# Three rotating buffers in place of two for the packed halves of f, q, k and k's gated product

## The chip, the cores and the metric

The kernel runs on one core of a Trainium2 chip. Its time is the device time of one execution in microseconds (us), as a median over several runs. Durations inside the kernel come from one profiled execution of the same program.

## The reference

The kernel computes a gated linear attention (B = 4 batches, H = 8 heads, S = 768 steps, D = 48 per head) and after it a layer norm and a two-layer MLP with a residual:

```python
f = 1.0 / (1.0 + np.exp(-f_logit))
for t in range(S):
    state = f[:, :, t, :, None] * state + np.einsum('bhd,bhe->bhde', k[:, :, t], v[:, :, t])
    y[:, :, t] = np.einsum('bhd,bhde->bhe', q[:, :, t], state)
x = y.transpose(0, 2, 1, 3).reshape(B, S, H * D)
xn = (x - mu) / np.sqrt(var + 1e-06) * g_ln
out = x + np.maximum(xn @ w_ch1, 0.0) @ w_ch2       # w_ch1: 384 x 1536, w_ch2: 1536 x 384
```

## The kernel before

The sequence is cut into NU = 12 units of T = 64 steps; a unit holds all four batches, so 256 tokens. For each unit n there is an attention part, `attention(n)`, and an MLP part, `mlp(n)`. No planner orders the work: the program runs through a plan written out by hand as a string of tokens, `START` for the first units and then `UNIT` once for each m from 3 to 11. Each token issues the instructions of one step, and each engine and each DMA queue executes its instructions in the order of the plan. An engine waits (on a semaphore) where an operand or a buffer is not ready; everything behind the waiting instruction on that engine waits too. A round of `UNIT` interleaves the MLP of unit m with the attention of unit n = m+1, the gates, q and k of unit o = m+2, and the fetching of unit p = m+3.

The matmuls need f, q and k with the head dimension across the partitions. The first three units do this with transposes on TensorE. From unit 3 on (`DIRECT = 3`) it is done by DMA, and a DMA transposition moves elements of 2 bytes, so each 4-byte number goes as two packed halves:

1. the raw tensor is loaded by DMA (`fraw`, or `kraw` for k and, in turn, for q);
2. `split(n, name, i, queue)`, line 420: ScalarE (ACT) copies one half of the rows (i = 0 or 1) into a tile `planes` (line 439), the low and the high 16 bits apart, and a DMA writes that tile to a DRAM tile, `{name}halves` (line 440). A token `p...` issues this DMA on GpSimd's queue (POOL), a token `P...` on SyncE's (SP);
3. `transfer(n, name)`, line 442, token `x...`: a DMA transposition on SP (line 454) brings both halves back from DRAM, turned, into `turned` (f and q share that tile) or into the tile named `qraw` (used for k). It waits for both writes.

The same is done with `kh`, k times its gates (name `K`), whose turned form `kt` the state update needs (`do_kt`).

So there are eight copies into `planes` in each round: two each for q, k, f and K. In the plan of a round their tokens are, in order: `p{p}f1`, `P{o}q0`, `p{o}q1`, `p{p}f0`, `p{p}k1`, `P{p}k0`, `p{o}K1`, `p{o}K0`. All take their tile from the pool `raws` under one tag, and with it one of that tag's buffers; a copy waits until the DMA that reads the buffer's former content has landed. The framework decides at build time which buffer a tile gets.

Around them, in the order of the plan on each engine: ACT also does the relus of `by_blocks` (line 962; the MLP's first product as blocks in DVE-made combinations), the copies of the attention's result into x (lines 816, 818), the copy of the first partial product p1 (line 1066), the sigmoid of the gates (line 695) and the scaled eviction of the transposed x (line 888). VectorE (DVE) adds partial products (lines 959, 1001, 1059), does the statistics (830, 831), the sums s1 to s4 of h (`sums`, lines 930 to 933), qh = turned q times the gates (725), kh (716), the normalization (875), the state (853) and kept, the state that is carried on (738). TensorE (PE) multiplies: `by_blocks` (line 951), then seven products p1, p2, p6, p5, p7, p3, p4 of the second layer (line 1051), with the transposes of x (886) ahead of p4, then the carried term of the next unit (`do_carried`, line 757, reads qh and kept), the scores (771), the values (807) and the state update (845). The one-bank PSUM tiles of all these rotate through four banks (`ps1`, bufs=4).

The third line of a round's plan, as an example:

```python
a{n}.chunk m{m} a{n}.stats m{m} x{o}q s{m} p{p}k1 P{p}k0 L{z}f a{o}.q a{o}.k m{m} x{p}f m{m}
```

Of the kernel before, what the change touches and what calls it, by code (L numbers as in the profile page):

```python
# [12 lines left out]
U16 = mybir.dt.uint16  # L13
# [314 lines left out]
def kernel(  # L328
# [20 lines left out]
    B, H, S, D = q.shape  # L349
    P = 128  # L350
# [31 lines left out]
    raws = fast.enter_context(tc.tile_pool(name="raws", bufs=2))  # L382
# [31 lines left out]
    def raw_of(n, name):  # L414

        return wide_heads["k" if n >= DIRECT and name == "q" else name]
# [3 lines left out]
    def split(n, name, i, queue):  # L420

        if n >= NU or n < DIRECT:
            return
        if (n, name) not in halved:
            halved[n, name] = drams.tile([P, 2, 2, 64 * H], U16, tag=f"{name}halves",
                                         name=f"{name}halves{n}")
        planes = raws.tile([P, 2, 64 * H], U16, tag="planes", name=f"{name}planes{n}_{i}")
        if name == "K":
            src = by_gates[n].rearrange("p (i s) t -> p i (s t)", i=2)[:, i].bitcast(U16).rearrange(
                "p (c two) -> p two c", two=2)  # L430
            to, there = planes, halved[n, name][:, :, i]
        else:
            src = raw_of(n, name).rearrange("p g h e -> p (g h e)")[
                :, i * D:i * D + (H - 1) * R * D + 64]
            src = bass.AP(tensor=src.tensor, offset=src.offset,
                          ap=[src.ap[0], [R * D, H], [1, 64]]).bitcast(U16).rearrange(
                              "p h (c two) -> p two h c", two=2)
            to, there = planes.rearrange("p two (h c) -> p two h c", h=H), halved[n, name][:, i]
        nc.scalar.copy(out=to, in_=src)  # L439
        queue.dma_start(out=there, in_=planes)  # L440
# [660 lines left out]
    def run(plan):  # L1101
        for token in plan.split():
# [8 lines left out]
            elif kind == "m":  # L1111
                if token not in running:
                    running[token] = mlp(int(rest))
                next(running[token])
            elif kind in "lL":
                queues = (nc.scalar if kind == "L" else nc.sync,)
                if rest[-1].isdigit():
                    load(int(rest[:-2]), rest[-2], (int(rest[-1]),), queues)
                else:
                    load(int(rest[:-1]), rest[-1], engines=queues)  # L1120
            elif kind in "pP":
                split(int(rest[:-2]), rest[-2], int(rest[-1]),
                      nc.sync if kind == "P" else nc.gpsimd)
            elif kind == "x":
                transfer(int(rest[:-1]), rest[-1])
            elif kind == "h":
                if token not in running:
                    running[token] = first_half(int(rest[0]), int(rest[1]))
                next(running[token])
            elif kind == "s":  # L1130
                sums(int(rest))
            elif kind == "y":
                if FIRST <= int(rest) < NU:
                    sums_of_x(int(rest))
            else:
                {"r": read, "w": write, "f": fetch, "t": mix, "d": idle,
                 "T": lambda: mix(nc.gpsimd), "u": mix_step,
                 "U": lambda: mix_step(nc.gpsimd)}[token]()
# [54 lines left out]
```

## Time and profile before

| what | value |
|---|---|
| time, median of 3 runs | 434.49 us (433.64 to 435.8) |
| profiled execution: its span | 434.5 us |
| TensorE busy (PE), its weight loads (PEld) | 415.5 us, 387.1 us |
| VectorE (DVE), ScalarE (ACT), GpSimd (POOL) busy | 332.9, 214.6, 121.8 us |
| mean granted TensorE clock | 0.987 |
| copies into planes (line 439) | 18 each for f, q, k and K, about 1.04 us each |
| DMA, all queues | 71.68 MB, mean 165 GB/s |

PE and PEld are one engine's matmuls and weight loads, which overlap. Matmuls are pipelined and their ends are modelled. An engine that is idle lost something only if it is on the path that sets the end. In the lists of waits the column after `<-` names what ended the wait; "issue" stands where the profile shows nothing that was waited for. SPq, ACTq and POOLq are the sequencers that issue DMAs.

### The profile page before, as it was taken

The numbers are of one execution on the slowest core, as the hardware profiler recorded it, in microseconds if no ns is written. First come the engines' busy times: TensorE is split into PE (matmuls) and PEld (weight loads), VectorE is DVE, ScalarE is ACT, GpSimd is POOL, SyncE is SP. The second block draws the span as 40 slices with busy tenths as digits, with TensorE's granted clock in tenths as the row PEclk, the third lists the DMA queues.
The fourth block names the chain that finished last, engine by engine and source line by source line (L and its number), as shares of the span: only waits on it lengthen the run. The fifth ranks groups of instructions, "written<-read, shape, count | busy, mean of one in ns | idle before, by whom it ended". The sixth has DMA issues, their size and how long they took to land.

```text
span 434.5 us, 12953 instructions
## 1 busy us (share of the span) xinstructions
PE 415.5 (96%) x5429; PEld 387.1 (89%) x5429; DVE 332.9 (77%) x539; ACT 214.6 (49%) x364; POOL 121.8 (28%) x148
## 2 busy tenths in 40 slices
PE   5599999899999997999999999999999999999995
PEld 4589887667879987999999999999999999999995
DVE  5998797665886758879879879879979879665561
ACT  2484856442544435665564564564574462351320
POOL 2362453560024004304204205105106005013011
PEclk9699999999999999999999999999999999999999
DMA  9998978896967798888797797698695690401001
GB/s 169 286 222 178 238 234 207 195 223 168 195 139 180 160 187 175 211 211 179 191 214 168 193 218 176 179 217 182 179 216 149 169 171 26 111 2 24 16 9 33
DMA packets 167647, 71.68 MB, mean 165 GB/s; under 512 B 151760, under 2 KB 157840, under 8 KB 167584
## 3 DMA queue, kind: packets, MB, share of 16 engines
q1 hardware_dynamic: 151728, 54.38, 58.5%
q0 software_dynamic: 3872, 12.64, 8.5%
q10 hardware_dynamic: 11984, 3.79, 4.2%
q8 instruction: 44, 0.72, 0.7%
q14 instruction: 19, 0.16, 0.1%
HBM read 28.31 MB, written 23.59 MB: 119 GB/s over the span
## 4 chain that ended last, share of the span: by engine, by line
PE 80%; DVE 6%; issue 5%; DMA 2%; POOL 2%; SPq 2%; ACT 2%; ACTq 0%; POOLq 0%; DVEq 0%
PE pp L1051 27%; PE bx L951 10%; PE by L951 9%; PE ph L1022 7%; PE ph L900 4%; PE po L1032 4%; PE bz L951 3%; PE shared L771 2%; PE py L757 2%; PE py L807 2%; PE bw L951 2%; PE bv L951 2%; PE xp L886 2%; PE shared L845 2%; DMA qhalves<-qplanes 1%
## 5 line engine op out<-in xcount | busy, mean ns | idle before, releaser
L962 ACT ACTIVATE h<-h 128x512 f32<-128x512 f32 x45 | 28.2, 630 | 42.2 <-DVE h L959 36.5
L1051 PE MATMUL pp<-mixed,s 128*128 128x192 f32 x240 | 40.7, 326 | 2.4 <-DVE s L931 2.4
L1051 PE MATMUL pp<-mixed,h 128*128 128x192 f32 x240 | 42.4, 326 | 0.0
L1051 PE MATMUL pp<-w,h 128*128 128x192 f32 x240 | 41.1, 327 | 1.1 <-ACT h L962 1.1
L1051 PEld LDWEIGHTS pp<-mixed,s 128*128 128x128 f32 x240 | 39.2, 190 | 2.6 <-issue 2.6
L1051 PEld LDWEIGHTS pp<-w,h 128*128 128x128 f32 x240 | 38.9, 190 | 1.7 <-ACT h L962 1.4
L1051 PEld LDWEIGHTS pp<-mixed,h 128*128 128x128 f32 x240 | 39.1, 190 | 0.1
L959 DVE TENSOR_TENSOR h<-h,bx 128x512 f32<-128x512 f32 x36 | 24.6, 683 | 17.1 <-PE bx L951 16.4
L439 ACT COPY Kplanes<-kh 128x1024 uint16<-128x1024 uint16 x18 | 18.2, 1045 | 37.8 <-DVE kh L716 26.4
L888 ACT ACTIVATE xt<-xp,gain 128x128 f32<-128x128 f32 x72 | 19.9, 373 | 31.5 <-PE xp L886 31.5
L668 DVE TENSOR_TENSOR_SCAN after<-gates,ends 128x1040 f32<-128x1040 f32 (+1 forms) x13 | 29.8, 2290 | 6.0 <-ACT gates L699 3.4
L1032 PE MATMUL po<-w,h 128*128 128x384 f32 x96 | 32.3, 489 | 0.0
L1022 PE MATMUL ph<-xt,w 128*128 128x256 f32 x144 | 31.9, 380 | 0.0
L440 POOL DMA_DIRECT2D qhalves<-qplanes x9 | 4.9, 545 | 96.5 <-ACT qplanes L439 96.5
L1022 PEld LDWEIGHTS ph<-xt,w 128*128 128x128 f32 x144 | 27.1, 190 | 4.1 <-ACT xt L888 0.3
L951 PE MATMUL bx<-y,v 128*128 128x128 f32 x216 | 28.7, 275 | 0.0
L680 DVE TENSOR_TENSOR_SCAN upto<-gates,starts 128x1040 f32<-128x1040 f32 (+1 forms) x13 | 28.1, 2158 | 0.5
L1032 PEld LDWEIGHTS po<-w,h 128*128 128x128 f32 x96 | 17.8, 190 | 11.3
L951 PEld LDWEIGHTS bx<-y,v 128*128 128x128 f32 x216 | 26.4, 192 | 0.1
L833 POOL TENSOR_SCALAR rstd<-mv 128x2 f32<-128x2 f32 (+1 forms) x13 | 8.1, 626 | 62.2 <-DVE mv L831 61.9
L439 ACT COPY fplanes<-fraw 128x1024 uint16<-128x1024 uint16 x18 | 18.9, 1054 | 8.9 <-DMA qhalves<-qplanes 6.6
L439 ACT COPY kplanes<-kraw 128x1024 uint16<-128x1024 uint16 x18 | 18.2, 1044 | 9.1 <-DMA kraw<-in_k_dram 4.4
(172 smaller groups left out, 955.3 us busy)
## 6 DMA issues: line engine op xcount, KB each, us to landing
w_0words<-in_moe_w_ch_dram SPq DMA_DIRECT2D x7, 768.0 KB, 5.1
v<-in_v_dram SPq DMA_DIRECT2D x46, 96.0 KB, 3.8
Khalves<-Kplanes POOLq DMA_DIRECT2D x16, 256.0 KB, 3.6
kraw<-in_k_dram SPq DMA_DIRECT2D x40, 96.0 KB, 3.8
fhalves<-fplanes POOLq DMA_DIRECT2D x14, 256.0 KB, 3.8
kraw<-in_q_dram SPq DMA_DIRECT2D x36, 96.0 KB, 3.1
fraw<-in_f_logit_dram ACTq DMA_DIRECT2D x27, 96.0 KB, 2.9
khalves<-kplanes POOLq DMA_DIRECT2D x9, 256.0 KB, 3.9
```

The lines of the kernel that those rows point to most:

```text
L439: nc.scalar.copy(out=to, in_=src)
L668: nc.vector.tensor_tensor_scan(out=at["after"].rearrange(flat)[:, c0:c1][:, ::-1], data0=gt[:, c0 + 1:c1 + 1][:, ::-1], data1=ends.rearran ...
L680: nc.vector.tensor_tensor_scan(out=at["upto"].rearrange(flat)[:, c0:c1], data0=gt[:, c0:c1], data1=starts.rearrange(flat)[:, c0:c1], initi ...
L757: nc.tensor.matmul(py[half(b ^ r), r, e * D:(e + 1) * D], lhsT=qh[head_rows(r), 2 * e + b], rhs=kept[head_rows(r), b, e], start=e == 0, st ...
L888: nc.scalar.mul(out=xt[:, m, g * P:(g + 1) * P], in_=pt[:, m], mul=gain[:, m:m + 1])
L900: nc.tensor.matmul(ph[:, j], lhsT=w1[:, m, (i + j) * P:(i + j + 1) * P], rhs=xt[:, m, tokens], start=m == 0, stop=m == KD - 1)
L951: nc.tensor.matmul(banks[bank][:, i], lhsT=right[:, i * P:(i + 1) * P], rhs=left, start=new and i == 0, stop=True, skip_group_check=True)
L959: nc.vector.tensor_tensor(out=out[to], in0=out[to], in1=bank, op=op)
L962: nc.scalar.activation(out=out[to], in_=out[to] if bank is None else bank, func=AF.Relu)
L1022: nc.tensor.matmul(ph[:, j], lhsT=w1[:, m, (i + j) * P:(i + j + 1) * P], rhs=xt[:, m], start=m == 0, stop=m == KD - 1)
L1032: nc.tensor.matmul(po, lhsT=h[:, i, g * P:(g + 1) * P], rhs=w2[:, i], start=i == 0, stop=i == KF - 1)
L1051: nc.tensor.matmul(pp, lhsT=a[:, i], rhs=b[:, i], start=i == 0, stop=i == KH - 1)
```

## The change

The tile `planes` of line 427 gets its own number of buffers, three, where the pool's two held before. No instruction, transfer or order in the plan is changed. One buffer is 2 x 512 numbers of 2 bytes in each of 128 partitions.

```diff
-        planes = raws.tile([P, 2, 64 * H], U16, tag="planes", name=f"{name}planes{n}_{i}")
+        planes = raws.tile([P, 2, 64 * H], U16, tag="planes", bufs=3,
+                           name=f"{name}planes{n}_{i}")
```

## The prediction

> **What bounds the kernel now.** I read the page's busy shares first, then the stretches of the span by engine, then the chain that ended last, then who waited for whom, and last the timeline of the one place that these point to. Busy time by engine, and the stretches (columns: length, then busy time and instructions of PE, PEld, DVE, ACT, POOL, then clock, DMA share, GB/s):
>
> ```profile
> PE 415.5 (96%) x5429; PEld 387.1 (89%) x5429; DVE 332.9 (77%) x539; ACT 214.6 (49%) x364; POOL 121.8 (28%) x148
> ...
> 80.00:140.00 60.00, 58.87 (x620) 46.67 (x619) 43.94 (x64) 26.86 (x44) 20.14 (x22) 1.00 0.79 185
> 140.00:168.38 28.38, 24.88 (x412) 22.73 (x410) 18.76 (x32) 14.33 (x22) 4.13 (x6) 1.00 0.91 170
> 168.38:400.71 232.33, 232.32 (x3253) 228.66 (x3254) 190.21 (x322) 119.31 (x203) 61.80 (x83) 1.00 0.69 163
> ```
>
> From 168.38 to 400.71 us PE is idle for 0.01 us. Whatever ACT waits for in that stretch costs nothing, because PE never runs out of work. ACT's waits can only matter where PE has a hole, and the one hole of size that lies after the first planes copies is in 140 to 168.38: 28.38 - 24.88 = 3.50 us. The chain that ended last (start, length, what) goes through that hole:
>
> ```profile
> 155.21 6.21 DMA qhalves<-qplanes
> ...
> 168.38 8.04 PE pp L1051 x48
> ...
> 177.07 1.95 PE pp L1051 x12
> ```
>
> So the write of a q half to DRAM carries the time of the whole kernel for 6.21 us. The waits (who <- whom: us in total, times, longest) say what stood behind it:
>
> ```profile
> PE pp L1051 <- DVE s L931: 2.4, 1, 2.4
> PE pp L1051 <- ACT h L962: 1.1, 1, 1.1
> PEld pp L1051 <- issue: 2.6, 1, 2.6
> PEld pp L1051 <- ACT h L962: 1.4, 1, 1.4
> ACT fplanes L439 <- DMA qhalves<-qplanes: 6.6, 1, 6.6
> ACT Kplanes L439 <- DMA khalves<-kplanes: 8.6, 2, 4.7
> ```
>
> PE lost 2.4 + 1.1 = 3.5 us in two waits (its weight loads, which stop first, 2.6 + 1.4 = 4.0), once each. ACT's single 6.6 us wait, for a buffer of planes, is the cause: the relu (L962) and the sums s wait behind it. The timeline of unit m=3 on all engines shows the order:
>
> ```profile
> 144.25 0.56 POOL L440 DMA_DIRECT2D fhalves<-fplanes  x1 [2.59 <-ACT fplanes L439]
> ...
> 153.88 1.04 ACT L439 COPY qplanes<-kraw 128x1024 uint16<-128x1024 uint16 x1
> 154.15 0.53 SPq L440 DMA_DIRECT2D qhalves<-qplanes  x1
> 155.21 0.54 POOL L440 DMA_DIRECT2D qhalves<-qplanes  x1 [10.40 <-ACT qplanes L439]
> 157.54 2.02 SPq L474 DMA_DIRECT2D kraw<-in_k_dram  x4
> 161.44 3.25 SPq L454 DMA_TRANSPOSE turned<-qhalves  x1
> 161.50 1.04 ACT L439 COPY fplanes<-fraw 128x1024 uint16<-128x1024 uint16 x1 [6.58 <-DMA qhalves<-qplanes]
> 162.84 0.54 POOL L440 DMA_DIRECT2D fhalves<-fplanes  x1 [7.08 <-ACT fplanes L439]
> 164.96 0.56 DVE L830 BATCH_NORM_STATS2 stats<-x 128x6 f32<-128x384 f32 x1 [4.42 <-ACT x L818]
> 167.30 1.04 ACT L439 COPY kplanes<-kraw 128x1024 uint16<-128x1024 uint16 x1 [1.24 <-issue]
> 169.89 1.61 DVE L725 TENSOR_TENSOR qh<-turned,upto 128x1024 f32<-128x1024 f32 x1
> ```
>
> I call the copies of this unit f1, q0, q1, f0, k1, k0 in ACT's order. f0 could start at 154.92 (q1's copy ends) and starts at 161.50. The DMA issues give the time to landing (last column), of f1's write (issued 144.25), q0's, q1's, then f0's and the transposition of q:
>
> ```profile
> fhalves<-fplanes POOLq DMA_DIRECT2D x1, 256.0 KB, 3.3
> ...
> qhalves<-qplanes SPq DMA_DIRECT2D x1, 256.0 KB, 3.6
> ...
> qhalves<-qplanes POOLq DMA_DIRECT2D x1, 256.0 KB, 6.2
> ...
> fhalves<-fplanes POOLq DMA_DIRECT2D x1, 256.0 KB, 4.4
> turned<-qhalves SPq DMA_TRANSPOSE x1, 6.0
> ...
> turned<-fhalves SPq DMA_TRANSPOSE x9, 4.3
> ...
> turned<-qhalves SPq DMA_TRANSPOSE x9, 5.5
> ```
>
> q0's write landed at 154.15 + 3.6 = 157.75, q1's at 155.21 + 6.2 = 161.4. f0 went at 161.50, so its buffer was the one that q1 had just filled, not the older one. f1's write had landed at 144.25 + 3.3 = 147.6.
>
> **The change part by part.** It adds one buffer of 128x1024 uint16, 2 KB in each partition. It adds and removes no instruction, no DMA and no byte, and changes no engine's order. No wait is added: a copy into planes waits for an older write than before, or for the same one. So everything is in the waits.
>
> First, f0. With three buffers, q0 and q1 hold two and the third is f1's, free since 147.6. f0 starts at 154.95 in place of 161.50. Its write follows on POOL 0.3 us after the copy (162.84 against 162.54 in the rows), so at about 156.3 in place of 162.84. On POOL it stands behind q1's issue (over at 155.75) and ahead of nothing until rstd, after the statistics. Its 256 KB now travel beside the k loads (SP, 157.54) and behind q1's write in POOL's own queue, not beside the transposition of q.
>
> Second, what this frees. Unit m=4 runs the same program without the wait, so it is the ruler:
>
> ```profile
> 160.54 1.47 PE L1051 MATMUL pp<-w,h 128*128 128x192 f32 x8
> 163.13 2.87 PE L1051 MATMUL pp<-w,h 128*128 128x192 f32 x16 [1.12 <-ACT h L962]
> 168.38 4.14 PE L1051 MATMUL pp<-mixed,s 128*128 128x192 f32 x24 [2.38 <-DVE s L931]
> ...
> 178.96 1.15 PE L757 MATMUL py<-kept,qh 48*64 48x48 f32 x64
> ...
> 196.53 4.07 PE L1051 MATMUL pp<-w,h 128*128 128x192 f32 x24
> ...
> 210.94 1.15 PE L757 MATMUL py<-kept,qh 48*64 48x48 f32 x64
> ```
>
> ```profile
> 190.81 1.05 ACT L439 COPY fplanes<-fraw 128x1024 uint16<-128x1024 uint16 x1
> ```
>
> From the first product p1 to the next carried term (L757), unit 3 takes 178.96 - 160.54 = 18.42 us and unit 4 takes 210.94 - 196.53 = 14.41. The difference, 4.01, is the hole as the weight loads see it. In unit 4, f0's copy starts 5.72 us ahead of p1; in the new unit 3 it would start 160.54 - 154.95 = 5.59 ahead: the same place. So the most that can be had is 4.0 us, with the carried term at 174.95.
>
> Third, what is late next. In unit 3 the transposition of q waits for q1's landing, which nothing here moves, so it is still issued at 161.44, while PE's work moves up past it. DVE's qh needs it, and kept, the last thing that the carried term needs, stands behind qh on DVE:
>
> ```profile
> 201.36 1.62 DVE L725 TENSOR_TENSOR qh<-turned,upto 128x1024 f32<-128x1024 f32 x1
> ...
> 208.71 0.95 DVE L738 TENSOR_TENSOR kept<-state,total 128x768 f32<-128x768 f32 x1
> ```
>
> From qh's start to kept's end it is 209.66 - 201.36 = 8.30 us. DVE itself would be ready for qh at 160.54 + (201.36 - 196.53) = 165.37. The landing is bounded by 4.3 us (the other transposition into the same tile) and 6.0 (this very transfer, with f0's write beside it): 165.7 to 167.4. I take 5.5, the median of its kind, since f0's write is now out of its way: 166.94. Then kept ends at 175.24, and the carried term starts there instead of 178.96: 3.7 us gained. At 6.0 it is 175.74 and 3.2; at 166.65 or earlier nothing is left to wait for and it is 4.0.
>
> At that transfer a rule can be weighed. f0's write and the transposition landed 0.2 us apart (162.84 + 4.4 against 161.44 + 6.0). The Trainium skill, DMA: Bandwidth & Descriptors, section Queues, rings and completion order, says that a completion's semaphore write lands only after every earlier write of that DMA engine, across its queues. The two landings agree with it but do not prove it. By that rule the transposition was held up by f0, would now come at its 4.3, and the kernel at 430.5.
>
> Fourth, all other planes copies. ACT's other waits on these buffers (8.6 us for Kplanes, the largest) fall between 80 and 140, where PE lacks 1.13 us in all, or in the full stretch after 168.38. I cost them at nothing; PE's queue of matmuls hides them, and if that cover were gone a copy would be worth at most its own wait. From the carried term on, PE runs without a hole to 400.71, so 3.7 us at 179 are 3.7 at the end, if unit 4 does not find its own transfers late; its q copies stand in ACT's order and move up with it.
>
> The sum: 434.5 - 3.7 = 430.8 us. The profiled span, 434.5, is also the median of the runs shown, 434.49 (433.64 to 435.8).
>
> **The rivals.** *No change.* The wait row shows that a copy does not simply get the oldest buffer: f0 got the newest, with the slower landing. If it got q1's again, nothing moves: 434.5. Against it: f1's buffer has been free for 7 us at that point, and even q0's (157.75) would do, since from f0 to the statistics ACT needs 164.96 - 161.50 = 3.46 us, so 161.2, which delays DVE by less than the wait for q does. *The k loads take its place.* k1's copy waited 1.24 us at 167.30 for something that the page calls issue. If that was the k load (issued at 157.54) and not f0's landing at 167.24, then k1, k0 and ACT's copy of p1 behind them stay where they are, and p1's PSUM bank is free only at about 169.5. Four banks hold p1, p2, p6 and p5; p7 is due at 160.54 + 4 x 1.95 = 168.3 and would be 1.2 late: carried at 176.15, 2.8 gained, 431.7. Against it: 167.24 and 167.30 fit too well, and with three buffers k1 no longer needs f0's. *Slower.* f0's 256 KB go out while q1's write, the k loads and the transpositions are under way. If that holds up the transposition of q, all of DVE stands behind it. The break-even is a landing at 178.96 - 8.30 = 170.66, 9.2 us after its issue; slower by 0.5% needs 11.4. At 12 us the carried term would start at 181.7 and the kernel end at 437.3. Against it: none of the landings quoted is over 6.2.
>
> **How the numbers follow.** Forecast 0.60: 430.8, its own range 430.0 to 432.0 (the landing's bounds, 430.5 to 431.3, and half a microsecond or so of run to run spread). k loads 0.12: 431.7. No change 0.20: 434.5 with the spread of the runs. Slower 0.06: about 437. Other 0.02. A measurement of this kernel tells about 0.5% (2.2 us) from nothing. Faster by over that: the forecast almost whole and most of the k case, 0.68; within it 0.26; slower 0.06. To hold 8 in 10, the range takes the first two cases and the lower half of no change: 429.8 to 434.6.
>
> **What would show it.** Right: f0's copy starts within 0.1 us of q1's copy's end; the 6.6 us row of ACT is gone; PE's two waits on pp (2.4 and 1.1) are gone or under 0.5; unit 3 from p1 to the carried term takes 14.4 to 15.3 us; from there on the times are those of before less the gain; qh is the one that waits, for the transposition of q. Wrong: f0 still waits for a q write; or k1 becomes ACT's long wait; or a hole of the same size opens further on, in unit 4, where PE has none now; or the first p1 is no longer at about 160.5, which would mean that the copies between 80 and 140 were not free.

## The result and the profile after

The changed kernel takes 431.85 us (median of 22 runs) against 435.19 us (median of 22 runs of the kernel before, on the same chip): a ratio of 0.994, interval 0.9916 to 0.9963 (the medians are over all runs; the ratio leaves out those that were disturbed and is not the quotient of the two medians, which is 0.9923). The forecast was 430.8 us, with a range of 429.8 to 434.6.

In the changed kernel every line from 428 on has a number one higher (the copy into planes is L440, its write L441, the products L1052, the carried term L758). The profiled execution took 431.19 us, of which its span is 429.4. First the busy row of its page, and the row of the chain that ended last, by engine:

```profile
PE 414.6 (97%) x5429; PEld 386.7 (90%) x5429; DVE 335.2 (78%) x539; ACT 214.2 (50%) x364; POOL 120.7 (28%) x148
...
PE 88%; ACT 3%; DVE 2%; SPq 2%; DMA 2%; issue 1%; POOL 0%; ACTq 0%; DVEq 0%; POOLq 0%
```

The same row of the kernel before, for comparison:

```profile
PE 80%; DVE 6%; issue 5%; DMA 2%; POOL 2%; SPq 2%; ACT 2%; ACTq 0%; POOLq 0%; DVEq 0%
```

Each engine has about as much to do as before (PE 415.5 us, now 414.6; DVE 332.9, now 335.2); PE's part of the chain has grown from 80% to 88%. The stretches of the span (length, then busy time and instructions of PE, PEld, DVE, ACT, POOL, then clock and DMA) show where:

```profile
80.00:140.00 60.00, 59.52 (x622) 47.12 (x621) 46.94 (x65) 27.35 (x45) 19.65 (x22) 1.00 0.86 190
140.00:164.36 24.36, 24.36 (x412) 22.91 (x412) 19.23 (x31) 14.65 (x22) 5.39 (x8) 1.00 0.91 196
164.36:395.90 231.54, 231.49 (x3252) 227.97 (x3251) 188.25 (x321) 118.52 (x202) 59.54 (x81) 1.00 0.70 162
```

The stretch with the hole, 28.38 us with PE busy for 24.88 of it, is now 24.36 us with PE busy for all of it, and holds the same 412 matmuls. The timeline of unit m=3 shows that the cause is gone. The first fence is PE (the carried term, then p1 and the last product, then the next carried term); the second is ACT, the queues and DVE around the copies:

```profile
142.17 1.15 PE L758 MATMUL py<-kept,qh 48*64 48x48 f32 x64
...
159.75 4.07 PE L1052 MATMUL pp<-w,h 128*128 128x192 f32 x24
163.65 4.06 PE L1052 MATMUL pp<-mixed,s 128*128 128x192 f32 x24
...
174.15 1.15 PE L758 MATMUL py<-kept,qh 48*64 48x48 f32 x64
```

```profile
151.47 0.53 SPq L441 DMA_DIRECT2D qhalves<-qplanes  x1
...
153.09 1.04 ACT L440 COPY qplanes<-kraw 128x1024 uint16<-128x1024 uint16 x1
154.02 1.05 ACT L440 COPY fplanes<-fraw 128x1024 uint16<-128x1024 uint16 x1
154.42 0.54 POOL L441 DMA_DIRECT2D qhalves<-qplanes  x1 [11.79 <-ACT qplanes L440]
154.46 2.09 SPq L475 DMA_DIRECT2D kraw<-in_k_dram  x4
155.36 0.54 POOL L441 DMA_DIRECT2D fhalves<-fplanes  x1 [0.41 <-ACT fplanes L440]
157.69 3.09 SPq L455 DMA_TRANSPOSE turned<-qhalves  x1
161.33 1.05 ACT L440 COPY kplanes<-kraw 128x1024 uint16<-128x1024 uint16 x1 [0.44 <-DMA kraw<-in_k_dram]
...
164.58 1.61 DVE L726 TENSOR_TENSOR qh<-turned,upto 128x1024 f32<-128x1024 f32 x1
```

f0's copy (154.02) follows q1's (153.09) with no wait in brackets; it had waited 6.58 us. From p1 to the next carried term it is 174.15 - 159.75 = 14.40 us, where it was 18.42: the whole 4.0. One thing was not foreseen: the transposition of q is issued at 157.69, not at 161.44. It waits for q1's write, and the landings (last column) of that write and of the transposition show what changed:

```profile
qhalves<-qplanes POOLq DMA_DIRECT2D x1, 256.0 KB, 3.3
...
turned<-qhalves SPq DMA_TRANSPOSE x1, 5.2
```

q1's write, the same 256 KB from the same queue, took 3.3 us and not 6.2. SP's queue was ahead at this time, and on that queue stands the write of another copy, that of K (k times its gates), which no longer waited. Before, then after:

```profile
131.72 1.05 ACT L439 COPY Kplanes<-kh 128x1024 uint16<-128x1024 uint16 x1 [3.83 <-DMA khalves<-kplanes]
132.79 0.59 SPq L440 DMA_DIRECT2D Khalves<-Kplanes  x1
```

```profile
128.19 1.04 ACT L440 COPY Kplanes<-kh 128x1024 uint16<-128x1024 uint16 x1
129.25 0.59 SPq L441 DMA_DIRECT2D Khalves<-Kplanes  x1
```

SP issued K's write 3.5 us earlier, q0's 2.7 earlier (151.47 against 154.15) and the k loads 3.1 earlier (154.46 against 157.54); 0.8 of each is that the whole round began earlier (142.17 against 142.96). That the earlier queue is what shortens q1's write is not shown by this. So the two profiles left three questions. How large is the hole, as profile and runs disagree (4.0 us against 0.6%, 2.6 us)? Is f0's buffer the cause by itself, or does the early K copy carry part of it? And does the third buffer lose something elsewhere, for example in the opening?

### The profile page after: what moved, and what is told of

It reads as the page before. It is cut to its first block, busy times and chain, and to the rows that moved or that the text cites. A ratio compares the mean times of both kernels' runs of the same rounds, so it can differ in the third digit from the quotient of the medians.

```text
span 429.4 us, 12958 instructions
## 1 busy us (share of the span) xinstructions
PE 414.6 (97%) x5429; PEld 386.7 (90%) x5429; DVE 335.2 (78%) x539; ACT 214.2 (50%) x364; POOL 120.7 (28%) x148
## 4 chain that ended last, share of the span: by engine, by line
PE 88%; ACT 3%; DVE 2%; SPq 2%; DMA 2%; issue 1%; POOL 0%; ACTq 0%; DVEq 0%; POOLq 0%
PE pp L1052 32%; PE bx L952 11%; PE by L952 10%; PE ph L1023 7%; PE po L1033 5%; PE bz L952 4%; PE ph L901 3%; PE py L808 2%; PE py L758 2%; PE shared L772 2%; PE bw L952 2%; PE bv L952 2%; SPq L475 2%; PE xp L887 2%; PE shared L846 2%; DMA kraw<-in_k_dram 1%
## 5 line engine op out<-in xcount | busy, mean ns | idle before, releaser
L1052 PE MATMUL pp<-mixed,h 128*128 128x192 f32 x240 | 42.4, 326 | 0.0
L1052 PE MATMUL pp<-w,h 128*128 128x192 f32 x240 | 40.8, 326 | 0.0
L1052 PE MATMUL pp<-mixed,s 128*128 128x192 f32 x240 | 40.6, 326 | 0.0
L1052 PEld LDWEIGHTS pp<-mixed,s 128*128 128x128 f32 x240 | 39.3, 190 | 0.0
L1052 PEld LDWEIGHTS pp<-w,h 128*128 128x128 f32 x240 | 38.9, 190 | 0.3
L1052 PEld LDWEIGHTS pp<-mixed,h 128*128 128x128 f32 x240 | 39.1, 190 | 0.1
L440 ACT COPY Kplanes<-kh 128x1024 uint16<-128x1024 uint16 x18 | 18.2, 1047 | 29.0 <-DVE kh L717 25.2
L441 POOL DMA_DIRECT2D qhalves<-qplanes x9 | 4.9, 545 | 98.4 <-ACT qplanes L440 98.4
L440 ACT COPY kplanes<-kraw 128x1024 uint16<-128x1024 uint16 x18 | 18.3, 1047 | 9.1 <-DMA kraw<-in_k_dram 6.0
L563 POOL TENSOR_TENSOR w<-w_0upper,w_0units 128x768 int32<-128x768 int32 x7 | 14.6, 2082 | 28.6 <-DVE w_0upper L561 28.6
```

The lines of the kernel that those rows point to most:

```text
L563: nc.gpsimd.tensor_tensor(out=to.bitcast(I32), in0=upper, in1=units, op=ALU.add)
L1052: nc.tensor.matmul(pp, lhsT=a[:, i], rhs=b[:, i], start=i == 0, stop=i == KH - 1)
```

## The experiments

In all of them the measure is the round of unit 3: from the carried term that opens it (that of unit 4, PE `py<-kept,qh` at 142 us or so) to the next one. In the changed kernel it is 174.15 - 142.17 = 31.98 us, with PE busy throughout. The kernel before had 36.0. What a round has over 31.98 is called its hole. In the kernels of the experiments the line numbers are one or two higher than before.

**Is the hole a constant?** Both kernels were run again unchanged: the one before three more times (one of them timed over several runs too), the one after three more times (two of them timed over several runs too).

> The kernel before, unchanged, for a second profile of it. Theory A (the hole of unit 3 belongs to the buffer that f0 is given): the 6.6 us wait of ACT and PE's waits of 2.4 and 1.1 us on pp are there again, and from p1 (L1051) to the carried term (L757) unit 3 takes about 18.4 us, within 0.5. Theory B (the hole hangs on how long q1's write takes, which varies from one execution to the next): the wait is of another size, between 2 and 7 us, and unit 3 takes 14.4 us plus 0 to 4.

> The kernel before against itself: what the comparison gives where nothing differs, and a third profile. Unit 3's round took 36.0 and 36.2 us in the two profiles, 4.0 to 4.2 over a round without a hole, but the timed gain of the change is 2 to 3.3 us. Theory C (the hole is of the same size every time, and the rest is the spread of the opening): 35.9 to 36.3 us again, and the moment of the first carried term of unit 4 (141.4 and 143.0 us before) scatters by a microsecond or more; ratio to itself within 0.997 to 1.003. Theory D (the hole varies, and the profiles happened to catch large ones): the round takes under 35 us in this profile or the next.

> A fourth profile of the kernel before. Theory C: unit 3's round 35.9 to 36.3 us. Theory D: under 35 us here or in the third.

The timeline's carried terms, the products with the sums s between them, ACT's wait (us in total, times, longest) and, last, the stretch of these products (columns as above, with the granted clock third from the end) in the first repetition:

```profile
141.44 1.15 PE L757 MATMUL py<-kept,qh 48*64 48x48 f32 x64
...
165.38 5.82 PE L1051 MATMUL pp<-mixed,s 128*128 128x192 f32 x24 [2.29 <-DVE s L931]
...
177.63 1.15 PE L757 MATMUL py<-kept,qh 48*64 48x48 f32 x64
...
ACT fplanes L439 <- DMA qhalves<-qplanes: 5.1, 1, 5.1
...
165.38:171.20 5.82, 5.82 (x26) 5.82 (x27) 5.82 (x9) 1.21 (x3) 2.87 (x4) 0.71 0.56 159
```

The carried terms and the waits of the second:

```profile
143.47 1.15 PE L757 MATMUL py<-kept,qh 48*64 48x48 f32 x64
177.14 1.15 PE L757 MATMUL py<-kept,qh 48*64 48x48 f32 x64
...
ACT fplanes L439 <- DMA qhalves<-qplanes: 4.3, 1, 4.3
PE pp L1051 <- DVE s L931: 1.5, 1, 1.5
```

And of the third:

```profile
143.00 1.15 PE L757 MATMUL py<-kept,qh 48*64 48x48 f32 x64
177.18 1.15 PE L757 MATMUL py<-kept,qh 48*64 48x48 f32 x64
...
ACT fplanes L439 <- DMA qhalves<-qplanes: 4.8, 1, 4.8
PE pp L1051 <- DVE s L931: 2.0, 1, 2.0
```

The rounds are 36.19, 33.67 and 34.18 us, and 36.00 in the profile that the prediction was made from. So the same program has a hole of 4.2, 1.7, 2.2 or 4.0 us, on average 3.0, and not one of a fixed size (theory D, not theory C). Not all of the 4.2 in the first repetition is waiting. There the 24 products with the sums took 5.82 us at a granted clock of 0.71; in the other three profiles they took 4.14 us at 1.00. That is 1.7 us, and no run here shows what lowered the clock. Without it the holes that come from waiting are 4.0, 2.5, 1.7 and 2.2 us, 2.6 on average. Their times were 435.17, 434.56 (median of 12; ratio against itself 0.9982, interval 0.9943 to 1.0021) and 435.97 us. With the clock set apart, f0's wait sets the hole: in each of the four profiles the hole is that wait (6.58, 5.09, 4.26 and 4.76 us) less 2.6 us, and in the three runs below in which f0 waits it is the wait less 2.5 or 2.6. So about 2.6 us of the wait cost nothing, and PE loses what lies beyond them.

> The changed kernel, unchanged, for a second profile and beside the one with a buffer for f0 alone, on one chip. Theory A: the round of unit 3 takes 31.98 us again, ratio to before 0.990 to 0.994, and the same as that of f0's own buffer within 0.2%. Rival (the earlier copies are worth something by themselves): it is faster than f0's own buffer by over 0.2%.

> The changed kernel again. Theory C: unit 3's round 31.98 us, the first carried term of unit 4 anywhere between 141 and 144.5 us, as in the kernel before. Rival E (three buffers slow the opening by about a microsecond, which takes back part of the 4.0): over all profiles the carried term of unit 4 comes 0.8 us or more later in the kernels whose opening has three buffers than in those with two. Ratio 0.991 to 0.996.

> A fourth profile of the changed kernel. Theory C: unit 3's round 31.98 us; the carried term of unit 4 between 141 and 144.5 us. Rival E: it comes late again, at 143.5 us or after.

The changed kernel gave 432.86 us (ratio 0.9955, 0.9921 to 0.9989), 433.76 (0.9943, 0.9911 to 0.9975) and 430.84 in a single execution; for the first the ratio was expected at 0.990 to 0.994. Its round was 31.98 or 31.99 us in all of its four profiles. The hole is what varies, and the third buffer takes away a wait of varying length.

The eight profiles divide as follows (us; the first carried term is that of unit 4 in the timeline, "six rounds" are those from the carried term of unit 5 to that of unit 11, the end is what follows it in the span):

| profile | first carried term | round of unit 3 | six rounds | the end | span |
|---|---|---|---|---|---|
| before, the one shown | 142.96 | 36.00 | 192.37 | 63.2 | 434.5 |
| before, again | 141.44 | 36.19 | 192.58 | 63.2 | 433.4 |
| before, third | 143.47 | 33.67 | 192.58 | 63.1 | 432.8 |
| before, fourth | 143.00 | 34.18 | 192.64 | 64.5 | 434.3 |
| after, the one shown | 142.17 | 31.98 | 192.10 | 63.2 | 429.4 |
| after, again | 143.91 | 31.99 | 191.94 | 63.2 | 431.0 |
| after, third | 141.47 | 31.99 | 192.10 | 63.1 | 428.7 |
| after, fourth | 142.01 | 31.98 | 191.97 | 63.1 | 429.1 |

The mean spans differ by 433.75 - 429.55 = 4.2 us: 0.3 at the first carried term, 3.0 in the round of unit 3 (0.4 of it the low clock of one profile), 0.5 in the six rounds, and 0.3 at the end, where a single profile has 1.3 more, behind PE's last matmul. The rival that three buffers slow the opening finds no support: the first carried term comes at 142.4 on average with three and at 142.7 with two, where 0.8 us or more later was expected. Both scatter by 2 us or more, so the difference of 0.3 between four and four says nothing, and a small effect either way is not excluded.

The runs give less than these spans: 2.0 to 2.6 us by the ratios. None of the profiled executions of the changed kernel (431.19, 432.72, 430.39, 430.84) lies above the median of its set, and the third is the lowest of 12 whose median is 433.76. What the longer runs lose is in no profile. The granted clock goes with part of it: in the third set the longest run, 436.39 us, had a mean of 0.978 and the shortest 0.986; but one of 434.49 us had 0.988, so the rest stays open.

**Is f0's buffer enough?** All tiles keep their two buffers, and f0 of unit 6, the one that waited, gets one of its own:

```diff
+        own = (n, name, i) == (DIRECT + 3, "f", 0)
+        planes = raws.tile([P, 2, 64 * H], U16, tag="ownplanes" if own else "planes",
+                           bufs=1 if own else 2, name=f"{name}planes{n}_{i}")
```

> Two buffers for all copies as before, and one of its own for the single copy f0 of unit 3 (the first half of f of unit 6). Theory A (f0's buffer is all that the third buffer changes): unit 3 from p1 to the carried term falls from 18.4 to 14.4 to 15.3 us; q1's write still lands about 6 us after its issue, so the transposition of q is issued about 1 us after p1 and qh waits for it; ratio to before 0.994, like the full change. Theory B (the earlier copies, which put SP's queue ahead, do it): SP stays where it was, q1's write still lands late, and the ratio stays within 0.998 to 1.002.

> Two buffers and one more for f0 of unit 3 alone, again, beside the full change on one chip. Theory A: round of unit 3 at 31.98 us, ratio within 0.2% of the full change's. Rival: slower than the full change by over 0.2%.

Rows of the timeline and of the landings, first run:

```profile
142.34 1.15 PE L759 MATMUL py<-kept,qh 48*64 48x48 f32 x64
154.19 1.05 ACT L441 COPY fplanes<-fraw 128x1024 uint16<-128x1024 uint16 x1
174.32 1.15 PE L759 MATMUL py<-kept,qh 48*64 48x48 f32 x64
...
qhalves<-qplanes POOLq DMA_DIRECT2D x1, 256.0 KB, 4.3
```

It took 431.36 us (ratio 0.9894, 0.985 to 0.9939, 6 runs) and, run again beside the changed kernel, 432.33 (0.9966, 0.9939 to 0.9992) where that had 0.9955. The round is 31.98 us in both profiles. K's copy still waited (2.69 us in the first), q1's write took 4.3 and 5.7 us, and it made no difference; theory B, by which the earlier copies do it, fails. So f0's own buffer removes the hole whole, and in time the two kernels can't be told apart. In the second run k1's copy waited 2.97 us for the k loads, and PE lost nothing; but it came 4.1 us after p1, where the prediction, with k1 6.8 us after p1, saw p7 late.

**What does the early K copy do?** There are three buffers here too, but the third is shared by three tiles alone: an early K copy, q1 and f0. So f0 must wait for q1's write, as before.

```diff
+        third = (n, name, i) in ((DIRECT, "K", 1), (DIRECT + 2, "q", 1), (DIRECT + 3, "f", 0))
+        planes = raws.tile([P, 2, 64 * H], U16, tag="third" if third else "planes",
+                           bufs=1 if third else 2, name=f"{name}planes{n}_{i}")
```

> The third buffer goes to the second half of K of unit 3 (the copy that waited 3.8 us in the opening) and later to q1 and f0 of unit 3 together, so that f0 still has to wait for q1's write, as before. Theory A (f0's buffer): f0 waits for q1's landing as before, unit 3 takes 17.5 to 18.4 us, ratio 0.998 to 1.002. Theory B (SP's queue ahead): K's copy goes about 3.8 us sooner, SP issues q0's write about 2 us sooner, q1's write lands in about 3.3 us in place of 6.2, f0 waits about 3.5 us in place of 6.6, and unit 3 takes 14.8 to 15.6 us; ratio about 0.995.

I had taken the wrong K: that of unit 3 is copied at about 90 us, and the one at 130.69 belongs to unit 4 and still waited 3.53 us. So it says nothing on an early K, but is a good control: three buffers in memory, f0 tied to q1. Timeline and waits:

```profile
159.85 1.04 ACT L441 COPY fplanes<-fraw 128x1024 uint16<-128x1024 uint16 x1 [6.73 <-DMA qhalves<-qplanes]
...
PE pp L1053 <- DVE s L933: 2.4, 1, 2.4
PE pp L1053 <- ACT h L964: 1.3, 1, 1.3
```

The hole is back, 36.15 - 31.98 = 4.2 us, with the two waits of PE that the kernel before had. The time is 435.12 us (0.9972, 0.9936 to 1.0008). With `(DIRECT + 1, "K", 1)` in the list, the K copy is the right one:

> The run with K tied gave the third buffer to the wrong K (of unit 3, at 92 us), so SP's queue was not ahead in it. Here it goes to the second half of K of unit 4, the copy at about 131 us that waits 3.5 to 3.8 us, and later to q1 and f0 together, so that f0 must still wait for q1's write. Theory A (f0's buffer is the cause; SP's queue matters little): f0 waits at least 5 us, and from one carried term to the next, the round of unit 3 takes 35.5 us or more (31.98 without a hole, 36.0 and 36.2 before). Theory B (SP's queue ahead makes q1's write land in about 3.3 us in place of 4.7 to 6.2): K's copy goes at about 128 us, f0 waits about 3.5 us, the round takes 32.3 to 33.5 us, ratio about 0.995.

```profile
130.06 1.04 ACT L441 COPY Kplanes<-kh 128x1024 uint16<-128x1024 uint16 x1
...
159.93 1.05 ACT L441 COPY fplanes<-fraw 128x1024 uint16<-128x1024 uint16 x1 [3.86 <-DMA qhalves<-qplanes]
...
PE pp L1053 <- DVE s L933: 1.1, 1, 1.1
...
qhalves<-qplanes POOLq DMA_DIRECT2D x1, 256.0 KB, 3.5
```

K didn't wait, q1's write took 3.5 us, f0 waited 3.86, and the round was 33.28: a hole of 1.3. In the profile that is what theory B forecast, and not theory A, which gave SP's queue little weight (a wait of at least 5 us, a round of 35.5 or more). In time it is 433.62 us, 0.998 (0.9951 to 1.001), where theory B had 0.995; the hole's 1.3 us, read from one profile, can't be told from the others in time. Over all profiles of kernels with two or three buffers q1's write took 3.2 to 3.8 us in the five where K had not waited, and 3.9 to 6.9 in the eight where it had. The ranges lie close together without overlapping, so the early K copy probably shortens that write; how it does so was not tried. It matters only while f0 depends on that write.

**Two buffers, strictly in turn.** f0 would then get q0's buffer, whose write is older:

```diff
+        by_gates["count"] = by_gates.get("count", 0) + 1
+        planes = raws.tile([P, 2, 64 * H], U16, tag=f"planes{by_gates['count'] % 2}", bufs=1,
```

> Two buffers as before, but dealt strictly in turn, so that f0 gets q0's buffer and not q1's. No more memory than before. If the choice of the buffer and not the number is what matters: f0 waits only for q0's write (landed 3.6 us after its issue), about 2.8 us in place of 6.6; the statistics come about 0.7 us late, which the transposition of q covers; unit 3 takes 14.4 to 15.3 us and the ratio is 0.994 like that of three buffers. If the number is what matters: unit 3 stays over 17 us and the ratio within 0.998 to 1.002.

```profile
158.22 1.04 ACT L441 COPY fplanes<-fraw 128x1024 uint16<-128x1024 uint16 x1 [3.53 <-DMA qhalves<-qplanes]
...
PE pp L1053 <- DVE s L933: 0.7, 1, 0.7
```

433.05 us, 0.9923 (0.9886 to 0.996, 9 runs). In the profile the wait is 3.53 us and the round 33.05, a hole of 1.1, and the next round has one of 1.0 (33.02), where all four profiles of the kernel before have 31.98. So part of the gain is to be had without memory. By its ratio it is no worse than three buffers, by its profile it is; a single profile of a wait that varies does not decide it.

**One buffer**, to see how far the rest of the program leans on the second:

```diff
-        planes = raws.tile([P, 2, 64 * H], U16, tag="planes", bufs=3,
+        planes = raws.tile([P, 2, 64 * H], U16, tag="planes", bufs=1,
```

> One buffer: each copy into planes waits for the landing of the write before it. It prices the cover in the full stretch, where the waits for two buffers cost nothing. f0 would start about 3.5 us later than with two (q1's write, issued 0.3 us after its copy, lands about 3 us later), which gives PE a hole of 0.5 to 1 us; k0 waits for k1's write, and ACT's copy of p1 behind it frees its PSUM bank about 4 us late. So 4 to 6 us a round in the eight rounds of the full stretch, and something in the opening: ratio 1.07 to 1.13. If the full stretch had slack for this too: under 1.02.

Five rounds in the full stretch, then the waits:

```profile
234.06:418.34 184.28, 166.64 (x2331) 160.67 (x2330) 132.59 (x225) 89.47 (x148) 39.99 (x57) 0.98 0.66 154
...
ACT Kplanes L440 <- DMA Khalves<-Kplanes: 26.6, 7, 4.5
ACT kplanes L440 <- DMA khalves<-kplanes: 26.2, 7, 5.2
ACT fplanes L440 <- DMA qhalves<-qplanes: 23.8, 6, 5.6
```

The same five rounds of the changed kernel:

```profile
206.13:366.25 160.12, 160.07 (x2331) 157.55 (x2331) 134.89 (x226) 87.40 (x146) 41.57 (x57) 1.00 0.78 177
```

483.42 us, 1.114 (1.1096 to 1.1185, 2 runs). A round takes 184.28 / 5 = 36.9 us on average in place of 32.0. Of these 4.8 us, 3.5 are idle time of PE; in the other 1.3 PE counts as busy for longer with the same 2331 matmuls, at a mean granted clock of 0.98 in place of 1.00. So the copies are not off the path by nature: one buffer costs 4.8 us a round; with two it is one hole in one unit and some tenths elsewhere; with three PE is idle for 0.05 us of the long stretch. The step from one to two had bought nearly everything. A fourth buffer was not run; the full stretch shows no idle time that it could take.

No run beat the changed kernel clearly; f0's own buffer equals it with the same memory.

## Why the prediction was right, and where it was off

- *Place and cause.* Right. f0 starts 0.1 us before q1's copy is over (154.02 against 154.13: the rows of the two copies overlap), ACT's wait and PE's two waits are gone, and the control with f0 tied to q1 brings all three back. The sign "the first p1 is no longer at about 160.5" came up, at 159.75; but the carried term ahead of it was as much earlier, 142.17 against 142.96, and that moment scatters by 2 us in one and the same program, so this sign says nothing.
- *The size at the place.* p1 to the carried term was forecast at 14.4 to 15.3 us and is 14.40. The forecast took off 0.3 us for the transposition of q, and that step was wrong: "the transposition of q waits for q1's landing, which nothing here moves". It moved from 161.44 to 157.69, so qh (164.58) found its operand there and 4.0 us were gained, not 3.7. The cause stands one step earlier in the same working, "All other planes copies … at nothing". For PE's time that holds (80 to 140 has 0.5 us of idle PE now, 1.1 before), but the K copy among them also sets when SP's queue moves on, and with it, probably, how long q1's write takes.
- *The rule on completion order.* The transposition landed in 5.2 us, neither 4.3 nor 6.0. f0's write was issued 2.3 us ahead of it this time (155.36 against 157.69) and landed 3.5 us ahead of it (155.36 + 4.0 = 159.4, against 162.9). In the third profile of the changed kernel the transposition took 6.0 us again, although f0's write had landed almost 4 us before it. So f0's write is not needed for the 6.0, and the 4.3 without it did not come. Whether other writes held the transposition is not shown, so the rule itself stays undecided.
- *The size in time.* The term that was mis-sized is the hole itself: 4.0 us "as the weight loads see it" in one profile, where waiting cost 4.0, 2.5, 1.7 and 2.2 us in four. By the ratios the timed gains are 0.6, 0.45 and 0.57%, that is 2.6, 2.0 and 2.5 us, below the 3.7 forecast. The mean of the four, 2.6 us (of 435, a ratio of 0.994), lies in the intervals of all three; 3.7 (0.9915) lies just outside the first two and inside the third.
- *The starting point.* "The profiled span, 434.5, is also the median of the runs shown" set a span equal to a time. In every run that has both, the time is 1.7 to 1.8 us more (431.19 against 429.4, 435.17 against 433.4), so an execution with a span of 434.5 should take about 436.2 us, longer than any of the three runs shown. That the two numbers agreed was chance, and a hole from a long execution was taken off a typical time. The forecast was 1.05 us under the measured 431.85: the kernel before has a median of 435.19 over 22 runs, 0.69 above the start of the sum, and the two medians differ by 3.34 us, 0.36 less than the 3.7 taken off.
- *The rivals.* No change: f0 got a free buffer. The k loads: k1 did wait for them, 0.44 us (and 2.97 in one run with f0's own buffer), and PE did not feel it. But k1 came 1.6 and 4.1 us after p1 there, and the price of 1.2 us for p7 supposed 6.8, so that price is untested. "167.24 and 167.30 fit too well" is weaker than it looked: in two repetitions of the kernel before, k1's wait (1.45 and 1.17 us) ended with a k load. Slower: the transposition landed in 5.2 us, where 9.2 was the break-even for an issue at 161.44.
- *What decides faster or same.* With a mean hole of 2.6 us and 0.5% at 2.2 us the change lies close to that limit; the ratios came out 0.45 to 0.6% under 1.

## What to carry to other kernels

Look for the holes of the engine that sets the end, follow each back to the wait that ends it, and use the same unit of the program where it has no hole as the ruler; here it told the round after the change to a hundredth. A wait of an engine off the path has a free part, here 2.6 us; only what lies beyond it is lost. How long a wait on a DMA landing lasts is a sample, so take its size from several profiles, look at the granted clock before a longer round is put down to waiting, and compare a span with a span and a time with a time. Which buffer a rotating tile gets counts, and not only how many there are, and a copy far off the path can still move a DMA queue, and with it, probably, a landing that is on it.

## What the runs showed of the hardware

The landing of one and the same write of 256 KB, issued by the same queue at the same place of the program, took 3.2 to 6.9 us over thirteen profiles, and 3.9 to 6.2 in four executions of one program. The shortest rounds took 31.98 us in every execution of every kernel with two or more buffers; others in which PE shows no idle time were up to 0.3 us longer (32.27 in the kernel before). So what scatters between these profiles is the opening (2.4 us between the first carried terms of the changed kernel's four), the waits on DMA landings, once a granted clock of 0.71 over 5.8 us behind such a wait (1.7 us lost, and none in the three other profiles of that program), and once the end behind PE's last matmul (1.3 us), and hardly the long stretch in which PE has work (its six rounds take 191.94 to 192.64 us).
